# Attention with a relative bias and a mixture of adapters: transposes as 64x64 quadrants, two equal value banks, another order of the work

## The chip, the cores and the metric

The kernel runs on one core of one Trainium2 chip. The time is the device time of one execution in microseconds (us); before the change the median of 3 runs was 206.64 us (206.42 to 207.58). TensorE is the engine for matrix products, VectorE and GpSimd are the engines for elementwise work, ScalarE is the one for exponentials and copies, SyncE issues transfers.

## What is computed

Eight batches of attention with eight heads, 576 positions and a head size of 64, with a bias that depends on the distance of two positions alone and is constant from distance 128 on. Then, for each of the 4608 rows of 512 values, a router picks two of eight adapters of rank 16 and adds their weighted outputs to the row.

```python
scores = scale * q @ k.T + bias_table[bucket(|i - j|)]
attn = exp(scores - max) ; attn = attn / (sum(attn) + 1e-09)
x = (attn @ v) reshaped to rows of 512            # batch, position, (head, d)
logits = x @ w_gate ; topk = the two largest
w = softmax(logits[topk])
out = x + sum over the two of w * ((x @ A[e]) @ B[e])
```

## The kernel before

**Tiling.** A unit is a batch and a pair of heads (`units`, L91); there are 32, four to a batch. Of the 576 positions 512 are the main part, 64 the tail. The 512 queries and keys lie in four chunks of 128, with the position modulo 4 naming the chunk (`load`, L103), so that a key chunk meets the same diagonal band of the bias in each query chunk.

**One unit.** `edges` (L374) makes the scores of tail keys against main queries (two whole-array matmuls, L381) and of main keys against tail queries (16 matmuls of 64x64 tiles, L389), in a tile of two banks, and one exponential (L392). `keys` (L332) makes the scores of one key chunk against 512 queries: four 64x64 tiles of 512 columns (L340), one for each head and each half of the chunk, then four that add the band of the bias (L345); `keys_exp` (L350) takes the exponential of the two banks. Score tiles rotate over three tiles of two banks (`score_tile`, L84). The bias of the edges is multiplied in afterwards (`edge_bias`, L395: GpSimd at L398, VectorE at L401). The values of a unit are made one unit later: `values_b` (L438) for query chunk 3 and the tail, `values_a` (L430) for query chunks 0 to 2; each has a bank of a ring of two (`mp`, L78). A query chunk takes 8 matmuls of 65 columns (64 values and a column of ones that gives the sum of the exponentials, L409) and one of 130 for the tail keys (L416); the tail takes 5 of 130 (L427). `normalise_a` and `normalise_b` (L457, L465) multiply by the reciprocal of the sums and write x.

**Transposes.** q and k of a unit are cast to bf16 (GpSimd, L144) and turned by eight 128x128 transposes into a bank of the ring of two (`transposes`, L297), copied out by VectorE (L305). Tail q and k go through `tail_transposes` (L309), x through `moe_x` (L484), the adapter's product z through `moe_t` (L551), each with a copy of its own.

**Adapters.** For each tile of 128 rows: the product with router and A (`moe_z`, L493), the gate (`moe_g`, `moe_w`, L521, L538; GpSimd and one tanh on ScalarE), the transpose of the gated z, the product with B and the addition of x (`moe_d`, L563, VectorE at L566), the store. A batch has four tiles of main rows, in two groups of two, and every two batches share a fifth for their tails. The adapters of a batch run during the next two batches' units, at places that `moe` (L599) writes down.

**Order.** The order is written out by hand; each engine runs its instructions in the order of the program. The loop over units (L695) emits: loads for unit u + 4 (SyncE), casts for u + 2 and v of u + 1 (`prep`, L666), `edges`, key chunks 0 and 2, an adapter product, `values_b` of u - 1, `values_a` of u - 1, key chunks 1 and 3, transposes of q and k of u + 2 (of u + 1 up to u = 3) and of x. The last unit and the remaining adapter tiles follow as written-out code (L789 on).

Of the kernel before, what the change touches and what calls it, by code (L numbers as in the profile page):

```python
# [14 lines left out]
ALU = mybir.AluOpType  # L15
# [23 lines left out]
def kernel(  # L39
# [34 lines left out]
    ep = ctx.enter_context(tc.tile_pool(name="probs", bufs=2))  # L74
    xp = ctx.enter_context(tc.tile_pool(name="x", bufs=3))
    ms = ctx.enter_context(tc.tile_pool(name="moe_sb", bufs=3))
    xtp = ctx.enter_context(tc.tile_pool(name="xT", bufs=4))
# [6 lines left out]
    def score_tile(name):  # L84
        return scps[next(turns) % 3].tile([128, 2, SM], FP32, name=name, tag="sc")


    TT = 2
    AHEAD = 3
# [5 lines left out]
    NV = 3  # L95
    vts = [cp.tile([128, 4, 2, W1], BF16, name=f"v{i}", tag=f"v{i}") for i in range(NV)]
    tvs = [cp.tile([128, HP, 2 * W1], BF16, name=f"vb{i}", tag=f"vb{i}") for i in range(2)]
    tls = [cp.tile([128, HP, 192], BF16, name=f"tl{i}", tag=f"tl{i}") for i in range(2)]
# [19 lines left out]
    def load_tail(b, names="qkv", g0=0, g1=HP):  # L118
        eng = nc.sync
        for nm in names:  # L120
            src = {"q": q, "k": k, "v": v}[nm][b, :, SM:, :]
            if nm == "v":
                t = stt.tile([128, HP, D], FP32, name="vt", tag="vt")
                for par in range(2):
                    eng.dma_start(out=t[par * 64:(par + 1) * 64, :, :],
                                  in_=src.rearrange("(g two) p d -> two p g d", two=2)[par])
# [20 lines left out]
    def cast_tail(b, nm, eng, g0=0, g1=HP):  # L147
# [6 lines left out]
        for par in range(2):  # L154
            rows = slice(par * 64, par * 64 + 64)
            eng.tensor_copy(tvs[b % 2][rows, :, par * W1:par * W1 + 64], tstage[(b, nm)][rows])
# [20 lines left out]
    for i in range(2):  # L177
        nc.vector.memset(tls[i], 0.0)
# [21 lines left out]
    ELC = cp.tile([128, HP * 192], BF16, tag="ELC")  # L200
    EL = ELC[:, :HP * 128].rearrange("p (g i) -> p g i", g=HP)
    EC = ELC[:, HP * 128:].rearrange("p (g i) -> p g i", g=HP)
    ET = cp.tile([128, HP, 2, 128], BF16, tag="ET")

# [18 lines left out]
    def factors_l():  # L223
        ps = score_tile("fl")
        for hp in range(HP):
            for e in range(2):
                for h in range(2):
                    rows = slice(h * 64, h * 64 + 64)
                    nc.tensor.matmul(_ap(ps[rows, 0, :], hp * 128 + e * 32, [[1, 32], [64, 2]]),
                                     lhsT=Wn[rows, hp, 129 - e:193 - e],  # L230
                                     rhs=turned(h), start=(hp == 0 and e == 0), stop=True,
                                     skip_group_check=True)
                    nc.tensor.matmul(_ap(ps[rows, 1, :], hp * 64 + e, [[2, 32]]),
                                     lhsT=Wn[rows, hp, 1 - e:65 - e],
                                     rhs=turned(h)[:, :32], start=(hp == 0 and e == 0), stop=True,
                                     skip_group_check=True)
        nc.scalar.activation(ELC, ps.rearrange("p a b -> p (a b)")[:, :HP * 192], ACT.Exp,
                             scale=scale)

    def factors_t():  # L240
        ps = score_tile("ft")
        pst = ps.rearrange("p h (g x) -> p h g x", x=64)
        for hp in range(HP):
            for e in range(2):
                for h in range(2):
# [5 lines left out]
        nc.scalar.activation(ET[64:].rearrange("p g c (h i) -> p h (g c) i", h=2), pst[64:], ACT.Exp,  # L251
                             scale=scale)

    def presets():
        for i in range(2):
            nc.gpsimd.memset(tvs[i], 0.0)
            nc.gpsimd.memset(pcs[i], 0.0)
        for i in range(2):
            nc.gpsimd.memset(tvs[i][:64, :, D:W1], 1.0)
            nc.gpsimd.memset(tvs[i][64:, :, W1 + D:], 1.0)  # L260
# [34 lines left out]
    qkT, probs, pva, pvb, xs, xe = ({} for _ in range(6))  # L295

    def transposes(u):  # L297
        ps = mp.tile([128, 2, 4, 128], BF16, name="tp", tag="mm")
        for i, nm in enumerate(("q", "k")):
            n = nat.pop((u, nm))  # L300
            for c in range(4):
                nc.tensor.transpose(ps[:, i, c, :], n[:, c, :, :].rearrange("p h d -> p (h d)"),  # L302
                                    ident)
        sb = qkp.tile([128, 2, SM], BF16, name="qkT", tag="qkT", bufs=3)
        nc.vector.tensor_copy(sb, ps.rearrange("p a c t -> p a (c t)"))  # L305
        qkT[u] = sb


    def tail_transposes(b, gr=None, g0=0, g1=HP):  # L309
        n = nat[(b, "qk")]  # L310
        ps = mp.tile([128, 2 * HP, 128], BF16, name="tq", tag="mm")
        for hp in range(g0, g1):
            nc.tensor.transpose(ps[:, hp, :], n[:, 2 * hp:2 * hp + 2, :].rearrange("p h d -> p (h d)"),
                                ident)
        if gr:
            for c in range(4):
                nc.tensor.transpose(ps[:, HP + c, :], gr.x[0][:, c * 128:(c + 1) * 128], ident)
        t = tls[b % 2][:, g0:g1, :]
        nc.vector.tensor_copy(t[:64, :, :128], ps[:64, g0:g1])
        nc.vector.tensor_copy(_ap(t[64:], 0, [[192, g1 - g0], [128, 2], [1, 64]]),  # L320
                              ps[64:, g0:g1].rearrange("p g (a i) -> p g a i", a=2))
        if gr:
            gr.xT = xtp.tile([128, 1, 4, 128], BF16, name="xT", tag="xT")
            nc.vector.tensor_copy(gr.xT, ps[:, HP:].rearrange("p (n c) t -> p n c t", n=1))  # L324

    def open_probs(u):
        probs[u] = (ep.tile([128, 4, 2, SM], BF16, name="pk", tag="pk"),
                    ep.tile([128, 2 * SM], BF16, name="pt", tag="pt"))

    scs, pcx = {}, {}  # L330

    def keys(u, c):  # L332
# [4 lines left out]
        halves = [(slice(h * 64, h * 64 + 64), slice(f * 64, f * 64 + 64), h, f)  # L337
                  for f in range(2) for h in range(2)]
        for rows, prt, h, f in halves:
# [3 lines left out]
        for rows, prt, h, f in halves:  # L343
            p0, n, y0 = (((0, 64, 32), (0, 96, 0)), ((32, 96, 0), (64, 64, 0)))[g][f]
# [3 lines left out]
        scs[c] = sc  # L348

    def keys_exp(u, c):  # L350
        nc.scalar.activation(probs[u][0][:, c, :, :], scs.pop(c), ACT.Exp, scale=scale)  # L351

    def corners(b, gr=None):
        pz = mp.tile([128, 512], FP32, name="ll", tag="mm")
        ps = pz[:, :HP * 64].rearrange("p (g i) -> p g i", g=HP)
        for hp in range(HP):
            t = tls[b % 2][:, hp, :]
            nc.tensor.matmul(ps[:, hp, :], lhsT=t[:, 64:], rhs=t[:, :64],
                             start=(hp == 0), stop=True, skip_group_check=True)
        if gr:  # L360
            moe_z(gr, 0, pz)
            moe_zc(gr, 0, pz)
            moe_g(gr, 0)
        pcx[b] = ep.tile([128, HP, 64], BF16, name="pcx", tag="pcx")
        nc.scalar.activation(pcx[b], ps, ACT.Exp, scale=scale)

    def corners_bias(b):
        px = pcx.pop(b)
        for h in range(2):
            rows = slice(h * 64, h * 64 + 64)  # L370
            nc.gpsimd.tensor_tensor(pcs[b % 2][rows, :, rows], px[rows], EC[rows], op=ALU.mult)


    def edges(u):  # L374
        b, hp = units[u]
        qT, kT = qkT[u][:, 0, :], qkT[u][:, 1, :]
        tl = tls[b % 2][:, hp, :]
        pt = probs[u][1]
        sc = score_tile("sc")
        for h in range(2):  # L380
            nc.tensor.matmul(sc[:, h, 256:], lhsT=tl[:, 64:],  # L381
                             rhs=_ap(qT, h * 64, [[128, 4], [1, 64]]), start=True, stop=True,
                             skip_group_check=True)
        for c in range(4):
            for f in range(2):
                for h in range(2):
                    rows = slice(h * 64, h * 64 + 64)
                    x0 = c * 128 + f * 64
                    nc.tensor.matmul(sc[f * 64:f * 64 + 64, h, c * 64:c * 64 + 64],  # L389
                                     lhsT=kT[rows, x0:x0 + 64], rhs=tl[rows, :64],  # L390
                                     start=False, stop=True, skip_group_check=True)
        nc.scalar.activation(_ap(pt, 0, [[64, 2], [128, 8], [1, 64]]),  # L392
                             sc.rearrange("p h (x i) -> p h x i", x=8), ACT.Exp, scale=scale)

    def edge_bias(u, eng=nc.vector):  # L395
        b, hp = units[u]
        tl = _ap(probs[u][1], SM + 96, [[128, 4], [1, 32]])
        nc.gpsimd.tensor_tensor(tl, tl, EL[:, hp, :].rearrange("p (c j) -> p c j", c=4),  # L398
# [649 lines left out]
```

## Time and profile before

| | |
|---|---|
| median of 3 runs | 206.64 us (206.42 to 207.58) |
| span of the profiled execution, first to last instruction | 204.3 us |
| granted TensorE clock, mean | 0.993 |
| busy: TensorE, VectorE, ScalarE, GpSimd | 181.9, 146.3, 164.8, 125.3 us |
| TensorE matmul records | 3682 |
| transferred | 39.72 MB, 194 GB/s on average |

The time of the profiled execution itself is not recorded; its span lies 2.3 us under the median, since the time of a run holds what goes before the first instruction and after the last as well. Rows of the profile name a line of the kernel, the engine, the operation, the tiles written and read, the number of instructions, and their busy time. TensorE's rows overlap, because matmuls are pipelined: the distance from one row's start to the next one's tells what a row takes of the engine. `PEld` are its weight loads.

### The profile page before, as it was taken

The numbers are of one execution on the slowest core, as the hardware profiler recorded it, in microseconds if no ns is written. First come the engines' busy times: TensorE is split into PE (matmuls) and PEld (weight loads), VectorE is DVE, ScalarE is ACT, GpSimd is POOL, SyncE is SP. The second block draws the span as 40 slices with busy tenths as digits, with TensorE's granted clock in tenths as the row PEclk, the third lists the DMA queues.
The fourth block names the chain that finished last, engine by engine and source line by source line (L and its number), as shares of the span: only waits on it lengthen the run. The fifth ranks groups of instructions, "written<-read, shape, count | busy, mean of one in ns | idle before, by whom it ended". The sixth has DMA issues, their size and how long they took to land.

```text
span 204.3 us, 8942 instructions
## 1 busy us (share of the span) xinstructions
PE 181.9 (89%) x3682; PEld 129.8 (64%) x3684; DVE 146.3 (72%) x453; ACT 164.8 (81%) x205; POOL 125.3 (61%) x319
## 2 busy tenths in 40 slices
PE   0477898999999989999999989999999899999850
PEld 0245666677767767776677767776677577777630
DVE  5322665677768787889788787888787878888850
ACT  3249688989998897998888879988998869789560
POOL 4293646933858573995849367978577639717020
PEclk9999999999999999999999999999999999999997
DMA  4859798867969487856377999955369932022176
GB/s 136 219 167 277 206 250 247 215 188 225 274 171 273 153 231 187 264 153 200 88 181 242 315 252 254 271 174 163 89 160 299 309 106 106 0 106 107 26 273 219
DMA packets 62113, 39.72 MB, mean 194 GB/s; under 512 B 17896, under 2 KB 59384, under 8 KB 62072
## 3 DMA queue, kind: packets, MB, share of 16 engines
q1 hardware_dynamic: 61272, 38.58, 64.0%
q10 hardware_dynamic: 800, 0.56, 1.1%
q8 instruction: 29, 0.48, 0.9%
q14 instruction: 12, 0.10, 0.2%
HBM read 29.67 MB, written 9.46 MB: 192 GB/s over the span
## 4 chain that ended last, share of the span: by engine, by line
PE 73%; DVE 10%; ACT 6%; DMA 4%; issue 2%; POOL 2%; ACTq 0%; POOLq 0%
PE pv L409 16%; PE sc L340 14%; PE tp L302 8%; PE sc L345 7%; ACT pk L351 5%; PE pv L427 4%; PE dl L565 4%; PE xT_ps L489 3%; PE pv L416 3%; PE pv L496 3%; PE sc L389 3%; PE sc L381 2%; DVE qkT L305 2%; DMA Wt<-g_d 1%; DMA g_d<-gp 1%
## 5 line engine op out<-in xcount | busy, mean ns | idle before, releaser
L351 ACT ACTIVATE pk<-sc 128x1024 bf16<-128x1024 f32 x128 | 124.1, 1027 | 20.8 <-PE sc L345 20.7
L340 PE MATMUL sc<-qkT 64*64 64x512 bf16 x512 | 52.1, 394 | 1.9 <-ACT pk L351 1.3
L409 PEld LDWEIGHTS <-pk 128*128 128x128 bf16 x1024 | 43.6, 98 | 8.7 <-DVE xT L324 2.7
L409 PE MATMUL pv<-v,pk 128*128 128x65 bf16 x992 | 45.5, 193 | 2.3 <-DVE xT L324 1.8
L345 PE MATMUL sc<-Wt,anti 64*64 64x256 bf16 (+1 forms) x512 | 44.1, 301 | 1.1 <-DMA Wt<-g_d 1.0
L392 ACT ACTIVATE pt<-sc 128x1024 bf16<-128x1024 f32 x32 | 32.7, 1023 | 5.1 <-PE sc L389 4.3
L305 DVE COPY qkT<-tp 128x1024 bf16<-128x1024 bf16 x32 | 22.1, 691 | 15.0 <-PE tp L302 14.6
L340 PEld LDWEIGHTS <-qkT 64*64 64x64 bf16 x512 | 18.1, 107 | 15.9 <-issue 5.3
L416 PE MATMUL pv<-vb,pt 128*128 128x130 bf16 x124 | 27.0, 218 | 0.0
L529 POOL TENSOR_TENSOR a<-z,top 128x16 f32<-128x16 f32 (+1 forms) x17 | 3.7, 220 | 34.8 <-DVE top L524 34.5
L144 POOL CAST kn<-ks 128x512 bf16<-128x512 f32 x31 | 19.4, 625 | 5.9 <-DMA ks<-in_k_dram 5.9
L566 DVE TENSOR_TENSOR ot<-dl,xn 128x512 f32<-128x512 f32 x24 | 16.6, 691 | 7.8 <-PE dl L565 7.4
L140 POOL CAST v<-vs 128x512 bf16<-128x512 f32 x32 | 19.9, 623 | 0.0
L345 PEld LDWEIGHTS <-anti 64*64 64x64 bf16 x512 | 18.1, 108 | 1.9 <-issue 1.8
L302 PE MATMUL tp<-ident,qn 128*128 128x128 bf16 x128 | 13.1, 227 | 5.9 <-ACT qn L144 4.9
L461 DVE TENSOR_TENSOR xn<-pv,rc 128x384 bf16<-128x384 f32 x31 | 17.3, 557 | 1.1
L144 POOL CAST qn<-qs 128x512 bf16<-128x512 f32 x27 | 16.5, 611 | 2.2 <-DMA qs<-in_q_dram 1.6
L302 PEld LDWEIGHTS <-qn 128*128 128x128 bf16 x128 | 7.6, 100 | 14.8 <-issue 7.1
L401 DVE TENSOR_TENSOR pt<-pt,ET 64x256 bf16<-64x256 bf16 x32 | 12.1, 377 | 5.0 <-ACT ET L251 3.9
L398 POOL TENSOR_TENSOR pt<-pt,ELC 128x128 bf16<-128x128 bf16 x32 | 13.7, 429 | 2.9 <-ACT pt L392 2.7
L477 DVE TENSOR_TENSOR xe<-pv,rc 64x64 bf16<-64x64 f32 x62 | 13.6, 219 | 0.6
L302 PE MATMUL tp<-ident,kn 128*128 128x128 bf16 x128 | 12.8, 225 | 0.9 <-POOL kn L144 0.9
(158 smaller groups left out, 339.3 us busy)
## 6 DMA issues: line engine op xcount, KB each, us to landing
qs<-in_q_dram SPq DMA_DIRECT2D x32, 256.0 KB, 4.6
vs<-in_v_dram SPq DMA_DIRECT2D x64, 128.0 KB, 3.7
ks<-in_k_dram SPq DMA_DIRECT2D x62, 128.0 KB, 3.8
out_dram<-ot SPq DMA_DIRECT2D x14, 512.0 KB, 3.3
vt<-in_v_dram SPq DMA_DIRECT2D x16, 64.0 KB, 2.9
out_dram<-fot SPq DMA_DIRECT2D x2, 512.0 KB, 3.4
qkt<-in_q_dram SPq DMA_DIRECT2D x7, 128.0 KB, 3.3
qkt<-in_k_dram SPq DMA_DIRECT2D x7, 128.0 KB, 3.6
```

Of the source, the lines that this page charges most:

```text
L140: eng.tensor_copy(t[:, :, :, :D].rearrange("p c h d -> p h c d"), s)
L144: copy(t.rearrange("p c h d -> p h c d"), s)
L302: nc.tensor.transpose(ps[:, i, c, :], n[:, c, :, :].rearrange("p h d -> p (h d)"), ident)
L305: nc.vector.tensor_copy(sb, ps.rearrange("p a c t -> p a (c t)"))
L340: nc.tensor.matmul(sc[prt, h, :], lhsT=kT[rows, c * 128 + f * 64:c * 128 + f * 64 + 64], rhs=qT[rows, :], start=True, stop=False, skip_gro ...
L345: nc.tensor.matmul(_ap(sc[prt, h, :], p0, [[128, 4], [1, n]]), lhsT=turned(h), rhs=_ap(Wt[rows, hp, :], (1 - e) * GY + y0, [[GY, 4], [1, n]]),
L351: nc.scalar.activation(probs[u][0][:, c, :, :], scs.pop(c), ACT.Exp, scale=scale)
L392: nc.scalar.activation(_ap(pt, 0, [[64, 2], [128, 8], [1, 64]]), sc.rearrange("p h (x i) -> p h x i", x=8), ACT.Exp, scale=scale)
L409: nc.tensor.matmul(pv[:, o + h * W1:o + (h + 1) * W1], lhsT=pk[:, c, h, t * 128:(t + 1) * 128], rhs=vm[:, c, h, :], start=(first and h == ...
L416: nc.tensor.matmul(pv[:, o:o + 2 * W1], lhsT=pt[:, SM + t * 128:SM + (t + 1) * 128], rhs=tvs[b % 2][:, hp, :], start=False, stop=False, sk ...
L461: nc.vector.tensor_tensor(_ap(xs[b], hp * 128, [[Dm, 3], [D, 2], [1, D]]), _ap(pv, 0, [[2 * W1, 3], [W1, 2], [1, D]]), _ap(rc, 0, [[2, 3], ...
L566: nc.vector.tensor_tensor(gr.ot[:, t, :], dl, gr.x[t], op=ALU.add)
```

## The change

Line numbers below are those of the kernel after.

- **Transposes** (`turn`, L354). Everything that has to be transposed at one place in a unit (q and k of unit u + 2, tail q and k of a batch, x tiles, gated z) goes into one list. A slot is a 128x128 block as four 64x64 quadrants, each a transpose of its own; up to 16 slots lie in one tile of two banks, which takes a turn of the three score tiles. One copy by VectorE brings all slots to SBUF, where ten such tiles rotate.
- **Edges** (L483). The tail keys against the main queries are four quadrants of 256 columns instead of two whole-array matmuls. The layout of the result changes, so VectorE's and GpSimd's bias products become `edge_t` and `edge_l`; a zero block of 64 columns ahead of each of three permanent tiles lets the tail's products take 128 columns.
- **Values** (L542). Two equal banks: `values(u, j)` makes query chunks j and j + 2, and the tail of head j of the pair as five matmuls of 65 columns. Reciprocal and normalisation are one operation each for a bank (L559, L560). Tail values are loaded and cast to both halves of the partitions.
- **Adapters.** Each row tile has its own store and its own fp32 output tile (8 of them). Groups for the gate are two tiles, or two and the tail tile. The z transposes ride in `turn`. The scores of the tail against itself (`corners`) lie in the free columns of a value bank.
- **Order** (L717). A unit is: loads, casts, `edges`, key chunks 0 and 2, adapter product and values j = 0 of u - 1, edge bias, key chunks 1 and 3, `turn` for u + 2 and the rest, values j = 1 of u - 1. q and k of u + 2 are turned in unit u from the first unit on. Tail loads and casts of a batch come up to two units earlier.
- **End** (L820 on). The last two units make their scores by halves of the queries (`keys_half`, L427: two key chunks against 256 queries) in an interleaved order; the last adapter tiles follow in a new written-out order. x is added for some of them by multiplying its transpose with the identity on TensorE, as before.

```diff
-    def score_tile(name):
+    def score_tile(name, shape=(128, 2, SM), dt=FP32):
+        return scps[next(turns) % 3].tile(list(shape), dt, name=name, tag="sc")
...
-                for par in range(2):
-                    eng.dma_start(out=t[par * 64:(par + 1) * 64, :, :],
-                                  in_=src.rearrange("(g two) p d -> two p g d", two=2)[par])
+                for f in range(2):
+                    eng.dma_start(out=t[f * 64:(f + 1) * 64], in_=src.rearrange("g p d -> p g d"))
...
+    def turn(items):
+        n = sum(k for _, k, _ in items)
...
+        ps = score_tile("tx", (128, 2, 1024), BF16)
+        sb = txp.tile([128, 16, 2, 64], BF16, name="tx", tag="tx")
+        s0 = 0
+        for _, k, src in items:
+            for i in range(k):
+                c = s0 + i
+                for a in range(2):
+                    for h in range(2):
+                        nc.tensor.transpose(ps[h * 64:h * 64 + 64, a, c * 64:c * 64 + 64], src(i, a, h),
+                                            ident[a * 64:a * 64 + 64, a * 64:a * 64 + 64])
+            s0 += k
+        nc.vector.tensor_copy(sb[:, :n], ps.rearrange("p a (c i) -> p c a i", i=64)[:, :n])
...
     def edges(u):
-        for h in range(2):
-            nc.tensor.matmul(sc[:, h, 256:], lhsT=tl[:, 64:],
-                             rhs=_ap(qT, h * 64, [[128, 4], [1, 64]]), start=True, stop=True,
+        for rows, prt, h, f in QUADS:
+            nc.tensor.matmul(sc[prt, h, 256:], lhsT=t[rows, 64:], rhs=qT[rows, f * 256:f * 256 + 256],
+                             start=True, stop=True, skip_group_check=True)
...
+    def pv_tail(u, pv, h, o=260):
...
+        for c in range(4):
+            x0 = 64 + h * SM + c * 64 - par * 64
+            nc.tensor.matmul(pv[:, o:o + W1], lhsT=probs[u][1][:, x0:x0 + 128], rhs=vts[u % NV][:, c, h, :],
+                             start=False, stop=False, skip_group_check=True)
+        nc.tensor.matmul(pv[:, o:o + W1], lhsT=pcs[par][:, hp, :], rhs=tvs[par][:, 2 * hp + h, h, :],
+                         start=False, stop=False, skip_group_check=True)
+
+    def values(u, j):
+        pv = mp.tile([128, 512], FP32, name="pv", tag="mm")
+        pv_main(u, pv, j, range(4))
+        pv_last(u, pv, j)
+        pv_tail(u, pv, j)
+        return pv
...
+    def normalise(u, j, pv):
...
+        nc.vector.reciprocal(rc[:, j, :5], _ap(pv, D, [[W1, 5]]))
+        nc.vector.tensor_tensor(xs[b][:, j, hp], _ap(pv, 0, [[W1, 5], [1, D]]),
+                                _ap(rc, 6 * j, [[1, 5], [0, D]]), op=ALU.mult)
...
+    tturn = {max(4 * c - 4, 2): c for c in range(1, B)}
+    tload = {max(w - 2, 0): c for w, c in tturn.items()}
...
+    for b in range(B - 1):
+        w = 4 * (b + 1)
+        for i in range(4):
+            at(xt, w + i, (x_item, b, i))
+            at(za, w + 1 + i, (b, i))
+            at(xt, w + 3 + 2 * (i // 2), (zt_item, b, i))
+            at(da, w + 4 + i, (b, i))
...
-    for u in range(NU - 1):
+    for u in range(NU - 2):
         open_probs(u)
         if u:
             prep(u)
+        if u in tload:
+            load_tail(tload[u])
...
         if u + 4 < NU:
             load(u + 4)
         edges(u)
         for c in KO[:2]:
             keys(u, c)
...
         if u:
...
+            step(u - 1, 0, da.pop(u, []), z=zs[0], zt=ta.pop(u, [None])[0])
...
+            edge_l(u)
+            edge_t(u)
         for c in KO[2:]:
             keys(u, c)
...
+        items.append(qk_item(u + 2))
+        if u in tturn:
+            items.append(tl_item(tturn[u]))
+        for fn, bb, i in xt.pop(u, []):
+            items.append(fn(tile_for(bb, i)))
+        turn(items)
         if u:
...
+            step(u - 1, 1, db.pop(u, []), z=zs[0], zt=tb.pop(u, [None])[0], corner=tcorner.get(u))
...
+    halves_of(U0, (0, 0), (0, 1))
+    step(U0 - 1, 0, [(L - 2, 2)], z=(L - 1, 1))
...
+    edges(U1)
+    halves_of(U1, (0, 0))
...
+    turn([x_item(T(L - 1, 2)), x_item(T(L - 1, 3))])
+    step(U0 - 1, 1, [(L - 2, 3)], z=(L - 1, 2))
...
+    halves_of(U1, (0, 1))
+    halves_of(U0, (1, 0))
+    step(U0, 0, [(L - 2, 4)], z=(L - 1, 3))
+    halves_of(U0, (1, 1))
+    halves_of(U1, (1, 0))
+    turn([zt_item(T(L - 1, 0)), zt_item(T(L - 1, 1))])
+    moe_w(groups[(L - 1, 2)])
...
+    halves_of(U1, (1, 1))
+    turn([zt_item(T(L - 1, 2)), zt_item(T(L - 1, 3)), x_item(T(L, 0)), x_item(T(L, 1))])
+    step(U0, 1, [(L - 1, 1)])
```

`step` emits the adapter products that are due, the values of a bank with router products and corner scores in its free columns, the normalisation, and the copies of what the bank holds besides.

More of the change, by code (lines that the diff above doesn't have):

```diff
@@ L309, in tail_transposes @@
-    def tail_transposes(b, gr=None, g0=0, g1=HP):
-        n = nat[(b, "qk")]
[L311 to L324, printed above, removed]
+    halves = (NU - 2, NU - 1)
@@ L633, with step @@
+    def step(u, j, ds=(), z=None, zt=None, corner=None):
+        for t in ds:
+            moe_d(tile_of(*t))
+        pv = values(u, j)
+        if z:
+            moe_z(tile_of(*z), pv)
+        if zt:
+            ps = moe_t(tile_of(*zt), pv)
+        if corner:
+            corners(*corner, pv)
+        normalise(u, j, pv)
+        if z:
+            moe_zc(tile_of(*z), pv)
+        if zt:
+            moe_tc(tile_of(*zt), ps)
     cast(0, "q", nc.scalar)
@@ L804 @@
+    step(U0, 1, [(L - 1, 1)])
+    zj = bank()
+    for i in range(2):
+        zsum(zj, i, T(L, i), range(HP), i == 0)
+    zcopy(groups[(L, 0)], zj, dve)
+    turn([x_item(T(L, 4)), x_item(T(L, 2), 0, 3), x_item(T(L, 3), 0, 3)])
+    s0 = next(turns)
     scx.close()
@@ L952 @@
-    rows4 = out[(B - 1) * S:(B - 1) * S + SM, :].rearrange("(p c) n -> p c n", c=4)
-    for i in range(2):
-        values(i, KO[3])
-    for i in range(2):
-        norm(i)
-    vx = turn(4, 1, bank(-1), (2, 3))
-    tall = turned16(bank(2), 2)
-    for t in range(2):
-        nc.tensor.transpose(tall[:, t, :], g1.zt[:, t, :, :].rearrange("p e r -> p (e r)"), ident)
-    act(g1.zT, tall)
-    z01, z23 = cut(bank(5), 2, ER + E), cut(bank(0), 2, ER + E)
-    for i in range(2):
-        zsum(z01, i, i, range(HP - 2))
```

954 lines of the change are left out of this document (408 added, 546 removed).

## The prediction

> **What bounds the kernel now.** First the page: span, busy shares, the chain by engine.
> ```profile
> span 204.3 us, 8942 instructions
> ...
> PE 181.9 (89%) x3682; PEld 129.8 (64%) x3684; DVE 146.3 (72%) x453; ACT 164.8 (81%) x205; POOL 125.3 (61%) x319
> ...
> PE 73%; DVE 10%; ACT 6%; DMA 4%; issue 2%; POOL 2%; ACTq 0%; POOLq 0%
> ```
> TensorE holds 73% of the chain that ends last; ScalarE is nearly as busy (81%) but holds 6%. The table by stretches comes next; I cut it where the score matmuls of units 5, 12, 16, 20, 24, 28 and 30 begin (a unit is a batch and a head pair, 0 to 31) and where the last exponential ends (189.08).
> ```profile
> core 0: us, PE busy (x) PEld busy (x) DVE busy (x) ACT busy (x) POOL busy (x), PEclk, DMA share, GB/s
> 41.31:78.50 37.19, 36.34 (x788) 26.66 (x786) 28.53 (x89) 33.36 (x40) 22.88 (x54) 1.00 0.75 213
> 78.50:100.48 21.98, 21.81 (x449) 15.31 (x447) 18.39 (x57) 19.93 (x26) 17.73 (x45) 1.00 0.61 190
> 100.48:122.40 21.92, 21.32 (x457) 15.59 (x455) 17.58 (x54) 18.89 (x24) 13.37 (x33) 1.00 0.82 235
> ...
> 144.37:166.29 21.92, 21.32 (x456) 15.59 (x455) 17.58 (x54) 18.87 (x24) 13.35 (x33) 1.00 0.78 223
> 166.29:177.92 11.63, 11.32 (x235) 8.16 (x232) 9.45 (x29) 10.88 (x14) 9.48 (x25) 1.00 0.12 48
> 177.92:189.08 11.16, 11.16 (x238) 7.99 (x236) 9.37 (x31) 9.68 (x13) 4.66 (x16) 1.00 0.25 98
> 189.08:204.30 15.22, 7.07 (x91) 5.04 (x89) 6.80 (x27) 6.07 (x16) 1.64 (x6) 0.90 0.50 174
> ```
> A batch of four units takes 21.92 to 21.98 us, 5.48 a unit, with TensorE busy 21.3 to 21.8 of it at the full clock and ScalarE 18.9 to 19.9. Units 5 to 28 take 166.29 - 41.31 = 124.98 us (5.43 each). So the middle is set by TensorE's own work. The start times of one unit on TensorE show what that work is (a row's second column is an overlapped duration; what counts is the distance from row to row):
> ```profile
> 100.48 0.38 PE L381 MATMUL sc<-qkT,tl 128*128 128x256 bf16 x2
> 100.80 0.32 PE L389 MATMUL sc<-tl,qkT 64*64 64x64 bf16 x16
> 100.94 0.39 PE L340 MATMUL sc<-qkT 64*64 64x512 bf16 x4
> 101.16 0.33 PE L345 MATMUL sc<-Wt,anti 64*64 64x256 bf16 x4
> 101.27 0.44 PE L340 MATMUL sc<-qkT 64*64 64x512 bf16 x4
> ...
> 101.75 0.39 PE L565 MATMUL dl<-Bc,zT 128*128 128x512 bf16 x1
> 101.98 0.42 PE L409 MATMUL pv<-v,pk 128*128 128x65 bf16 x8
> 102.24 0.22 PE L416 MATMUL pv<-vb,pt 128*128 128x130 bf16 x1
> 102.29 0.40 PE L427 MATMUL pv<-v,pt 128*128 128x130 bf16 x4
> ...
> 102.58 0.40 PE L496 MATMUL pv<-AW,xT 128*128 128x136 bf16 x4
> 102.92 0.42 PE L409 MATMUL pv<-v,pk 128*128 128x65 bf16 x8
> ...
> 103.86 0.22 PE L558 MATMUL pv<-ident,zt 128*128 128x128 bf16 x1
> 104.01 0.41 PE L340 MATMUL sc<-qkT 64*64 64x512 bf16 x4
> ...
> 104.84 0.40 PE L302 MATMUL tp<-ident,qn 128*128 128x128 bf16 x4
> ...
> 105.30 0.61 PE L489 MATMUL xT_ps<-ident,xn 128*128 128x128 bf16 x8
> 105.75 0.38 PE L381 MATMUL sc<-qkT,tl 128*128 128x256 bf16 x2
> ```
> Edge scores 0.46 (100.48 to 100.94), two key chunks 0.81 (to 101.75), adapter output 0.23, values and router 0.94 (to 102.92), values and one transpose 1.09 (to 104.01), two key chunks 0.83, transposes of q and k 0.46 (eight, 57 ns each), of x 0.45 (in two units of four). Two prices follow. A pass from whole-array to 64x64 work costs a pause: a whole-array matmul of 130 columns takes 0.055 (102.24 to 102.29), one of 128 from 103.86 to 104.01 0.15, so 0.09 is the pause. And 16 quadrant matmuls of 64 columns, each with a weight load of its own, take 100.80 to 100.94: 0.036 for four that lie side by side.
>
> ScalarE over the same unit:
> ```profile
> 101.22 1.02 ACT L392 ACTIVATE pt<-sc 128x1024 bf16<-128x1024 f32 x1
> 102.14 1.94 ACT L351 ACTIVATE pk<-sc 128x1024 bf16<-128x1024 f32 x2
> ...
> 104.62 1.94 ACT L351 ACTIVATE pk<-sc 128x1024 bf16<-128x1024 f32 x2 [0.55 <-PE sc L345]
> ```
> Five exponentials, 0.92 apart (101.22 to 102.14; 1.94 for two of 1.02), and 0.55 idle until TensorE delivers. The exponential of the chunk begun at 104.01 starts at 104.62, 0.26 after TensorE is through with it (chunk: 0.35).
>
> **The change part by part, per unit in the middle.** *Transposes.* One slot is four 64x64 quadrants in place of one 128x128. The nearest row is L389: same tile form, own weights in every quadrant, 64 columns, so 0.036 a slot against 0.057. L302's transposes cost what L416's plain matmul does (0.055), so a transpose has no price of its own. A unit turns 8 slots of q and k, 4 to 8 of x, and adapter and tail slots, 14.6 on average: 0.53, with 0.04 for the pass back 0.57. Taken away: 0.46 + 0.25 (4.5 of x) + 0.06 (zT) + 0.06 (tail). Bounds of a slot: 0.031 (64 columns at the pace of L409, 65 columns in 0.0325) and 0.107, one whole weight load:
> ```profile
> L340 PEld LDWEIGHTS <-qkT 64*64 64x64 bf16 x512 | 18.1, 107 | 15.9 <-issue 5.3
> ```
> Loads last 0.107, yet four with their matmuls take 0.036: they hide. The Trainium skill, TensorE: Matmul & The Clock Gate, section LDWEIGHTS (loading the stationary operand), gives a load columns / 1.2 ns, an estimated 53 ns for 64; a slot paced by it would make the unit 5.18 and the time about 200, by the row it is 194.3.
> *Edge scores.* Two whole-array matmuls of 256 columns become four quadrants beside each other: 0.11 (the L345 row of 256 columns, 101.16 to 101.27) instead of 0.31 with the pause in it; with 0.15 for L389 and the 0.09 pause 0.35. *Values.* Two equal banks: 16 x 0.0325 + 2 x 0.055 + 5 x 0.033 = 0.80 each; the tail products are ten of 65 columns instead of five of 130 (+0.05). With router (0.24) and pause the first is 1.13, the second 0.85 with corners and the tail's router. *Keys* stay: 0.81 and 0.79 (no pass behind the second pair). TensorE's sum: 0.35 + 0.81 + 0.23 + 1.13 + 0.79 + 0.57 + 0.85 = 4.73.
>
> *A new wait.* The transposes go to a two-bank tile of the ring of three score tiles, so six take turns: edges, c0, c2, c1, c3, turned tile. The turned tile takes c2's place and waits for c2's exponential. From the first edge matmul: edge exponential at 0.35 + 0.25 = 0.60; c2's starts 2 x 0.915 later and ends after 1.02; release 0.06: 3.51. TensorE alone would be there at 0.35 + 0.81 + 0.23 + 1.13 + 0.79 = 3.31. Behind the waiting transpose stand the second value bank and the next unit's edge scores, for which ScalarE waits: 3.51 + 0.57 + 0.85 = **4.93 a unit**. ScalarE's own sum is 5 x 0.915 + 0.19 (a tanh, half a corner exponential) = 4.77, so it doesn't bound, but it is the floor. I take 4.93; lower end 4.77.
>
> *VectorE.* A unit's copies out of transposes become one of 14.6 x 128 = 1870 elements, and four operations normalise it instead of six.
> ```profile
> L305 DVE COPY qkT<-tp 128x1024 bf16<-128x1024 bf16 x32 | 22.1, 691 | 15.0 <-PE tp L302 14.6
> L461 DVE TENSOR_TENSOR xn<-pv,rc 128x384 bf16<-128x384 f32 x31 | 17.3, 557 | 1.1
> L566 DVE TENSOR_TENSOR ot<-dl,xn 128x512 f32<-128x512 f32 x24 | 16.6, 691 | 7.8 <-PE dl L565 7.4
> ```
> At L305's rate (0.15 + 0.53 ns an element, the 0.15 as in the two fp32 rows) 1.13 us; against 0.69 + some 0.8 in the smaller copies now; with the two operations less VectorE's 18.39 / 4 = 4.6 a unit falls to an estimated 4.2, under 4.93. The copy ends 0.25 + 1.13 after the turn, the second bank's reciprocal and normalisation 0.67 after that: 0.3 before the next first bank wants its place. The corner exponential now reads that bank too and VectorE waits for it with the output additions behind; it is short of that 0.3, cost nothing while the cover lasts, at most 0.27 in two units of four.
>
> *GpSimd and DMA.* The tail's v is loaded and cast twice, outputs leave by tile. GpSimd is at 17.7 of 22 us at most, and its casts of q and k end before 3.5 in the unit; SyncE has waits to give:
> ```profile
> SPq L582 <- DVE rc L468: 33.9, 9, 11.4
> ```
> Counted as nothing; without that cover 16 further issues of 0.64 (L125's row, below) would be 10 us.
>
> *Start.* q and k of unit u+2 are turned at the end of unit u from the first unit on (now one unit later up to u = 3), so arrival counts:
> ```profile
> 27.52 0.61 POOL L144 CAST kn<-ks 128x512 bf16<-128x512 f32 x1 [2.98 <-DMA ks<-in_k_dram]
> ...
> 32.95 0.61 POOL L144 CAST kn<-ks 128x512 bf16<-128x512 f32 x1 [0.87 <-DMA ks<-in_k_dram]
> ...
> 36.41 0.61 POOL L144 CAST kn<-ks 128x512 bf16<-128x512 f32 x1
> ```
> k of units 4 and 5 is cast by 28.13 and 33.56: edge scores of units 3 and 4 not before 29.3 and 34.7 (cast, turn 0.3, values 0.85). The tail load of batch 2 now stands ahead of load 6, four issues of 0.64,
> ```profile
> 39.61 1.28 SPq L125 DMA_DIRECT2D vt<-in_v_dram  x2
> ```
> so k of unit 6 comes at 37.0 + 2.6 = 39.6, less what it lay ready (about 0.1), and unit 5 starts at 39.5 + 0.57 + 0.85 = 40.9 instead of 41.31. I take 0.4 gained; ends: 3 lost, 2 gained.
>
> *End.* Today unit 30's edges start at 177.92, the last exponential ends 11.16 later, the last addition (next row) at 198.07, +20.15, the span at +26.4.
> ```profile
> 197.38 0.69 DVE L1016 TENSOR_TENSOR fol<-f,xe 128x512 f32<-128x512 f32 x1 [0.27 <-PE f L916]
> ```
> New: the same ten exponentials, ending at +11.2 by the prices above. Then, as estimates from these prices: wait for the adapter's gate (tanh behind the ninth exponential, three GpSimd steps) to 11.2, ten slots, the last bank of unit 30 and router 2.4, second turn, outputs of batch 6 and routers 2.4, to 16.0; second half of unit 31 normalised, turned, routed 1.9, gate 1.5, turned and multiplied 1.2, copied 0.6; the tail tile behind it 1.2: +22.3. Stores 5.5 (6.2 now, with 512 KB pieces): +27.8, **1.4 lost**; ends 1 gained, 4 lost.
>
> *Sum.* 40.9 + 25 x 4.93 + 27.8 = 192.0 of span against 204.3. What lies around the span: median 206.64 less 204.3 is 2.3 (the runs reach from 206.42 to 207.58). 192.0 + 2.3 = **194.3 us**.
>
> **The rivals.** *ScalarE's floor*, if release and turn are shorter than I take them: 4.77, 25 x 0.16 = 4 less, 190.3. For it: only 0.16 apart. *Weight loads set the slot.* If a quadrant's load hides only half behind the quadrants before it (0.107 / 2), a slot is 0.053, a unit 4.93 + 14.6 x 0.017 = 5.18, the time 200.5; against it stands L389 with its 0.036. This is what the section on LDWEIGHTS above comes to.
>
> *The copy runs at the fp32 rate* (reads 64 elements from one bank, then from the other): (691 - 557) / 128 = 1.05 ns an element, 2.1 us. Then the loop turn, copy, normalise, next first bank, keys, turn is 0.53 + 0.25 + 2.1 + 0.67 + 0.06 + 1.92 = 5.53 a unit: 209.3. Against it: L305 reads the same type from PSUM.
>
> *Slower: the quadrants don't overlap their loads.* Place: every turn. Price: 0.107 a slot, the weight-load row; 4.93 + 14.6 x 0.071 = 5.97 a unit, 220.3. It decides from 0.07 a slot, where 12.3 us / 25 units is used up. For it: never is there a run of more than 16 quadrants in L389, and a turn has up to 64; against it: within the 16 no slowing is seen. The Trainium skill has a rule for this on the same page, section "Wait — 56ns, not 53.3ns?": however small, matmuls start no less than some 25 ns apart, an estimate of 100 ns a slot, with a time near this rival's. The trace disagrees: L389's 16 start within 0.15.
>
> **How the numbers follow.** Forecast 0.67; ScalarE's floor 0.10; half-hidden loads 0.07; slow copy 0.08; quadrants in a row 0.08. The likeliest gives 194.3. The range goes from the floor with an even end (188.5) to half-hidden loads with the worst start (204); that leaves out the last two cases and some of the rest. A measurement here tells 0.5% from nothing. Slow copy and quadrants come in degrees: of their 0.16 I count 0.02 faster, 0.03 within 0.5%, 0.11 slower. So faster 0.67 + 0.10 + 0.07 + 0.02 = 0.86, same 0.03, slower 0.11.
>
> **What would show it.** Right: slots of 0.031 to 0.04 in the turn, units of 4.8 to 5.05 us, TensorE waiting for ScalarE ahead of the turn, copies of 1.0 to 1.25, unit 5 near 41, about 28 us from unit 30 on. Wrong: slots over 0.05, copies near 2, TensorE waiting for VectorE ahead of a value bank, or for casts in the middle; an end of over 31 us.

## The result, and the profile after

The changed kernel takes **213.32 us** (median of 4 runs, 212.76 to 214.36), the kernel before 206.53 in the same comparison: a ratio of 1.033 (95% interval 1.029 to 1.037), slower by far more than the 0.5% that a measurement can tell. The forecast was 194.3, its range 188.5 to 204. Some runs fall into a slower state: the times and ratios below are of fast runs, but the profiles of e1_whole, e4_before_split and e9_fewer_elsewhere are of slow ones, 1.5 to 1.6% above the fastest of their kernel.

The profiled run took 213.37 us. From its page, the span, TensorE's line and the queue that brings instructions (packets, MB, share):
```profile
span 211.5 us, 12203 instructions
...
PE 171.7 (81%) x5399; PEld 132.6 (63%) x5399; DVE 129.6 (61%) x327; ACT 164.1 (78%) x204; POOL 124.0 (59%) x303
...
q8 instruction: 42, 0.69, 1.3%
```
Before, TensorE had 3682 matmuls and was busy 89% of the span; now it has 5399 and is busy 81%. Instructions come by DMA: 0.69 MB / 42 is 16 KB a packet, and 5399 matmuls with 5399 weight loads, each an instruction, are some 42 times 256; such 256 are called a block from here on. Before there were 29 packets for 3682 and 3684. The table by stretches, cut where the edge scores of units 5 and 30 begin:
```profile
42.26:182.43 140.17, 125.33 (x4085) 96.89 (x4084) 96.13 (x234) 122.34 (x151) 90.58 (x208) 0.99 0.70 204
182.43:211.50 29.07, 18.61 (x504) 14.47 (x501) 17.07 (x50) 13.94 (x23) 8.75 (x31) 0.95 0.33 111
```
The start took 42.26 (forecast 40.9), the middle 140.17 (25 x 4.93 = 123.25), the end 29.07 (27.8): 1.4, 16.9 and 1.3 over. So the miss lies in the middle, where TensorE stood still for 14.8 us (140.17 less 125.33; before 2.7). What it waited for, over the whole run (us in total, times, longest; "issue": nothing that the profile shows):
```profile
PE sc L422 <- issue: 4.7, 3, 2.5
PE sc L494 <- issue: 4.2, 3, 2.6
...
PE tx L365 <- ACT pk L425: 1.4, 4, 0.4
...
PE pv L520 <- issue: 1.2, 4, 0.4
PE sc L417 <- issue: 0.9, 1, 0.9
...
PE pv L520 <- DVE xn L560: 0.7, 2, 0.4
...
PE aw L285 <- issue: 0.6, 1, 0.6
```
Those on buffers and engines, which the prediction had thought of, are small. The issue rows that fall into the middle come to 12.1 us in 14 stops, with the smaller ones that aren't shown; the kernel before has none. The longest stop, in the order of instructions on TensorE (start, duration of the group; the bracket is the idle time before it):
```profile
106.40 0.30 PE L489 MATMUL sc<-tx 64*64 64x256 bf16 x4
106.53 0.22 PE L494 MATMUL sc<-tx 64*64 64x64 bf16 x5
109.31 0.28 PE L494 MATMUL sc<-tx 64*64 64x64 bf16 x11 [2.55 <-issue]
...
110.73 0.61 PE L616 MATMUL dl<-Bc,tx 128*128 128x512 bf16 x1
111.13 1.09 PE L520 MATMUL pv<-v,pk 128*128 128x65 bf16 x16
112.03 0.40 PE L528 MATMUL pv<-vb,pt 128*128 128x130 bf16 x2
```
The stretch behind the stop in the table by stretches (the clock stands behind the engines' columns):
```profile
109.31:113.10 3.79, 3.79 (x56) 2.62 (x56) 0.69 (x1) 2.86 (x3) 3.25 (x6) 0.55 0.32 97
```
TensorE stops in the middle of 16 like matmuls, all free to run: 5 are issued, then nothing for 2.55 us, then 11. Behind it the matmuls are slow as well: sixteen value products take 0.90 (111.13 to 112.03) where they take 0.51 elsewhere (100.24 to 100.75, below); the granted clock from 109.31 to 113.10 is 0.55. This isn't so behind every long stop: behind that of 2.48 us before 168.42 the clock was 1.00 (168.42 to 172.20). Where do the stops stand? The same table, cut at seven of them, counts the matmuls and weight loads in between:
```profile
69.17:86.00 16.83, 15.21 (x512) 11.73 (x513) 12.18 (x30) 14.54 (x18) 10.62 (x28) 1.00 0.84 246
86.00:109.31 23.31, 19.79 (x642) 15.31 (x642) 16.22 (x38) 19.58 (x24) 16.14 (x38) 1.00 0.77 215
109.31:127.74 18.43, 16.67 (x513) 12.93 (x514) 11.67 (x29) 15.75 (x19) 11.15 (x24) 0.91 0.67 191
127.74:141.39 13.65, 12.37 (x384) 9.31 (x385) 9.72 (x24) 12.52 (x15) 7.89 (x19) 1.00 0.73 210
141.39:163.05 21.66, 19.81 (x641) 15.13 (x642) 16.29 (x38) 18.84 (x24) 14.26 (x34) 1.00 0.74 217
163.05:168.42 5.37, 2.90 (x128) 2.43 (x129) 1.97 (x4) 3.21 (x5) 3.58 (x11) 1.00 0.74 228
```
Matmuls and loads together: 1025, 1284, 1027, 769, 1283, 257, which are 4, 5, 4, 3, 5 and 1 times 256, but for a few at the edges. Each stop is the end of a block of instructions: **the next one was not there yet**. In the trace's record of transfers the packet of that next block (1.0 us) starts 0.3 to 3.5 us after the block ahead was begun, 1.6 on the mean, and its instructions run 1.15 us after its end at the earliest. From the packet of 45.98 to that of 185.78, 32 further, a block takes 4.37 us; 327 instructions a unit (8169 in the row 42.26) / 256 x 4.37 = 5.58, the 5.61 measured. That counts the same blocks once more and proves nothing by itself; the experiments below do. Before it was one packet in 6.2 us.

### The profile page after: what moved, and what is told of

Same layout as the page of the kernel before. It is cut to its first block, busy times and chain, and to the rows that moved or that the text cites. A ratio compares the mean times of both kernels' runs of the same rounds, so it can differ in the third digit from the quotient of the medians.

```text
span 211.5 us, 12203 instructions
## 1 busy us (share of the span) xinstructions
PE 171.7 (81%) x5399; PEld 132.6 (63%) x5399; DVE 129.6 (61%) x327; ACT 164.1 (78%) x204; POOL 124.0 (59%) x303
## 5 line engine op out<-in xcount | busy, mean ns | idle before, releaser
L425 ACT ACTIVATE pk<-sc 128x1024 bf16<-128x1024 f32 x120 | 114.5, 1031 | 12.5 <-PE sc L422 12.3
L417 PE MATMUL sc<-tx 64*64 64x512 bf16 x480 | 50.9, 403 | 1.0 <-issue 0.9
L422 PE MATMUL sc<-Wt,anti 64*64 64x256 bf16 x480 | 43.4, 309 | 6.7 <-issue 4.7
L368 DVE COPY tx<-tx 128x2048 bf16<-128x2048 bf16 (+8 forms) x36 | 36.3, 1009 | 18.5 <-PE tx L365 18.1
L560 DVE TENSOR_TENSOR xn<-pv,rc 128x320 bf16<-128x320 f32 x62 | 30.5, 491 | 2.1
L559 DVE RECIPROCAL rc<-pv 128x5 f32<-128x5 f32 x62 | 11.9, 192 | 22.9 <-PE pv L567 13.7
L417 PEld LDWEIGHTS <-tx 64*64 64x64 bf16 x480 | 16.9, 109 | 10.8 <-issue 2.8
L365 PEld LDWEIGHTS <-qn 64*64 64x64 bf16 x512 | 11.1, 112 | 14.5 <-ACT qn L141 4.9
L537 PE MATMUL pv<-v,pt 128*128 128x65 bf16 x248 | 18.0, 195 | 0.2 <-issue 0.2
L528 PE MATMUL pv<-vb,pt 128*128 128x130 bf16 x124 | 17.5, 224 | 0.0
L494 PE MATMUL sc<-tx 64*64 64x64 bf16 x512 | 11.3, 196 | 4.2 <-issue 4.2
L537 PEld LDWEIGHTS <-pt 128*128 128x128 bf16 x256 | 14.2, 99 | 0.4 <-issue 0.4
```

The costliest lines, as they stand in the source:

```text
L365: nc.tensor.transpose(ps[h * 64:h * 64 + 64, a, c * 64:c * 64 + 64], src(i, a, h), ident[a * 64:a * 64 + 64, a * 64:a * 64 + 64])
L368: nc.vector.tensor_copy(sb[:, :n], ps.rearrange("p a (c i) -> p c a i", i=64)[:, :n])
L417: nc.tensor.matmul(sc[prt, h, :], lhsT=kT[rows, c * 128 + f * 64:c * 128 + f * 64 + 64], rhs=qT[rows, :], start=True, stop=False, skip_gro ...
L422: nc.tensor.matmul(_ap(sc[prt, h, :], p0, [[128, 4], [1, n]]), lhsT=turned(h), rhs=_ap(Wt[rows, hp, :], (1 - e) * GY + y0, [[GY, 4], [1, n]]),
L425: nc.scalar.activation(probs[u][0][:, c, :, :], sc, ACT.Exp, scale=scale)
L537: nc.tensor.matmul(pv[:, o:o + W1], lhsT=probs[u][1][:, x0:x0 + 128], rhs=vts[u % NV][:, c, h, :], start=False, stop=False, skip_group_che ...
```

## The experiments

*Theory:* the change put so many instructions into a unit that their blocks arrive late. *Rivals:* the long runs of transposing quadrants themselves hold TensorE; the waits between engines set the unit; every instruction has a price. Times stand beside the kernel before on the same chip.

**e1_whole.** One whole-array transpose a slot:
```
+    nc.tensor.transpose(ps[:, c, :], src(i, 0, None), ident)
-    for a in range(2):
-        for h in range(2):
-            nc.tensor.transpose(ps[h*64:h*64+64, a, c*64:c*64+64], src(i, a, h), ident[...])
```


> The changed kernel with one whole-array transpose a slot in place of four quadrants (in the few turns that hold a tail tile the quadrants stay; the heads of a value bank lie side by side so that a slot is one operand). TensorE has 8382 instructions in place of 10800. Theory (instructions arrive too late: blocks of 256, some 4.3 us apart at best): 262 instructions a unit take longer to run than to fetch, so the waits for nothing at every 256th instruction go, although the transposes themselves get dearer by 14.6 x 0.021 = 0.3 us a unit: units of 5.1 to 5.3, 200 to 206 us. Rival (the added waits between the engines set the unit, the missing instructions only follow): the unit grows by the 0.3, 214 to 221 us.

204.95 us, ratio 0.992 (0.989 to 0.995): 0.8% under the kernel before, 8 us faster than the change. Units of 5.22 (4.93 and the 0.3 of the dearer slots), 32 packets, and the waits for nothing are down to 0.3 us. The theory's figures came.

**e2_rows.** Two transposes of 64 rows by 128 columns a slot:
```
+    nc.tensor.transpose(ps[:, a, c*64:c*64+64], src(i, a, None), ident[pr, pr])
-    for h in range(2): ... (64 by 64)
```


> The changed kernel with two transposes of 64 rows by 128 columns a slot in place of four quadrants, into the same two banks (tail tiles keep quadrants). 9020 TensorE instructions in place of 10800, 282 a unit. Theory (late instructions): 282 instructions are fetched in some 4.7 us, under the unit's 4.93: nearly all waits for nothing go, 197 to 205 us. Rival (waits between engines): the columns, banks and copies are those of the changed kernel, so 211 to 215 us.

200.44 us, 0.972 (0.968 to 0.975). The middle, and eight slots in it behind the last bias (q from 71.97, k up to 72.20):
```profile
44.01:169.77 125.76, 119.28 (x3372) 92.68 (x3390) 96.63 (x234) 121.11 (x151) 90.39 (x208) 1.00 0.77 224
```
```profile
71.67 0.33 PE L426 MATMUL sc<-Wt,anti 64*64 64x384 bf16 x4
71.97 0.29 PE L366 MATMUL tx<-ident,qn 64*128 64x64 bf16 x8
...
72.20 0.30 PE L366 MATMUL tx<-ident,xn 64*128 64x64 bf16 x8
```
0.23 for eight, 0.029 a slot, like the quadrants' 0.031, with half the instructions. The middle takes 125.76, 5.03 a unit; waits for nothing fall to 0.8 us. The columns, banks and copies are those of the change, and so is the order of the work, so these don't make it slow.

**e3_noload.** `load` issues nothing for units over 5.

> The changed kernel; the loads of q, k and v of units 6 to 31 are left out (their casts read what units 2 to 5 loaded), all else is kept, all 10800 TensorE instructions too. If the instruction blocks come late because they queue behind the data: each block's packet starts within 0.8 us of the block before being taken up, and the waits for nothing vanish or fall under 2 us in all, 195 to 201 us. If the fetch is slow by itself: the packets start as late as before (1.4 us on the mean) and the waits stay, 207 to 214 us. If the waits between the engines set the unit: DMA waits are 1 us in all, 211 to 214 us.

202.95 us, 0.982 (0.977 to 0.988). All 10,800 instructions are there, yet the middle is 127.94 and the waits for nothing come to 3.0 over the run (12.5 in the change), the largest row being the one below:
```profile
43.01:170.95 127.94, 120.27 (x4065) 95.61 (x4084) 96.76 (x234) 121.41 (x151) 90.54 (x208) 1.00 0.23 70
```
```profile
PE sc L425 <- issue: 1.1, 2, 0.9
```
This lies between the first two expectations: counted by the weight loads, the packets start 1.1 us after the block ahead on the mean (1.6 in the change), and the late ones, up to 3.5, are gone (2.2 at most). Most of the loss needs the data traffic (70 GB/s here, 204 in the change); the fetch isn't quick without it.

**e4_before_split.** The other way round, in the kernel before:
```
+    for x in range(0, SM, SM // 4):
+        for rows, prt, h, f in halves:
+            nc.tensor.matmul(sc[prt, h, x:x+128], lhsT=..., rhs=qT[rows, x:x+128], ...)
-        nc.tensor.matmul(sc[prt, h, :], lhsT=..., rhs=qT[rows, :], ...)
```


> The kernel before with its key scores cut into smaller matmuls: four of 128 columns for each one of 512, two bias matmuls for each one; same columns, same results, no wait, copy or tile changed. TensorE has 11466 instructions in place of 7370, 358 a unit. Theory (late instructions): 358 / 256 blocks x 4.3 us = 6.0 us a unit in place of 5.43, waits for nothing at every 256th instruction, 215 to 228 us. Rival (waits between engines, instructions arrive in time): the same columns take the same time, 206 to 209 us.

218.27 and 219.48 us, 1.060 (1.055 to 1.065). A chunk's sixteen matmuls of 128 columns take 0.23 (84.28 to 84.51 in the trace), as four of 512 did, and still:
```profile
PE sc L342 <- issue: 3.5, 5, 1.3
PE pv L413 <- issue: 3.4, 3, 1.7
PE sc L349 <- issue: 2.6, 5, 0.7
```
The kernel before now has the change's fault without any part of the change, 383 matmuls and 383 loads from the stop at 85.2 to the one at 98.1 (three blocks). Units of 6.01. Stops make up 8.6 us of the 13.6 by which the middle is longer than before (150.17 against 136.61); the rest I only put down to what they upset, it wasn't taken apart.

**e5_keys_rows** and **e6_all_rows** take instructions out of the key scores, by tiles of 64 by 128:
```
+    for h in range(2):
+        nc.tensor.matmul(sc[:, h, :], lhsT=kT[rows, c*128:c*128+128], rhs=qT[rows, :], ...)
-    for rows, prt, h, f in QUADS: ... (64 by 64)
```


> The changed kernel with its turned tiles as they are (quadrants), but the key scores and the key half of the edge scores as products of 64 rows by 128 columns instead of pairs of quadrants: 9808 TensorE instructions, 306 a unit. Theory (late instructions, wherever they stand): 306 / 256 blocks x 4.1 to 4.4 us = 4.9 to 5.25 a unit, 199 to 207 us. Rival (long runs of transposing quadrants themselves hold TensorE up): the runs are as long as before, 211 to 215 us.

> The kernel of e2_rows (transposes of 64 by 128) with the key scores and the key half of the edge scores as 64 by 128 as well: 8028 TensorE instructions, 251 a unit. Theory (a threshold: instructions cost only where their blocks come late): e2_rows had no late block left, so 198 to 201 us, as e2_rows. Rival (every instruction has a price, as from the changed kernel to e2_rows 12.9 us for 1780 = 7 ns): 992 fewer give 7 us, 193 to 194 us.

214.43 (1.041, 1.037 to 1.045) and 216.10 us (1.048, 1.045 to 1.050): both outside the theory, the first within its rival's 211 to 215; yet hardly a stop is left (0 and 0.2 us in all), and the turn that the rival blames takes e5_keys_rows as long as the change (0.64 a unit up to the values behind it, on the mean). Two chunks of e6_all_rows, then of e2_rows:
```profile
102.38 0.39 PE L422 MATMUL sc<-tx 64*128 64x512 bf16 x2
102.70 0.36 PE L426 MATMUL sc<-Wt,anti 64*64 64x256 bf16 x4
102.99 0.39 PE L422 MATMUL sc<-tx 64*128 64x512 bf16 x2
```
```profile
71.11 0.41 PE L421 MATMUL sc<-tx 64*64 64x512 bf16 x4
71.35 0.33 PE L426 MATMUL sc<-Wt,anti 64*64 64x256 bf16 x4
71.46 0.44 PE L421 MATMUL sc<-tx 64*64 64x512 bf16 x4
```
A chunk takes 0.61 (102.38 to 102.99) instead of 0.35 (71.11 to 71.46): scores of 64 by 128 and bias of 64 by 64 now follow each other, with a pause at each pass from one tile form to the other. On the mean of units 5 to 29 it is 0.10 from scores to bias, four times a unit, and 0.18 from bias to the next scores, twice: 0.75 more a unit, some of it won back elsewhere, so that units take 5.57 and 5.61 where e2_rows has 5.03. The prediction had a price like that (0.09) for whole-array tiles and I didn't apply it here, so the pair says nothing between theory and rival.

**e7_rows_cast**, **e12_rows_cast_again.** In e2_rows TensorE waits in unit 4:
```profile
PE aw L285 <- POOL A L277: 2.8, 1, 2.8
```
The edit puts `weights_cast()` ahead of `prep(3)`.

> The kernel of e2_rows with the casts of the adapter's weights put ahead of unit 3's other casts on GpSimd (there TensorE waits 2.8 us for them in unit 4, as they stand behind a cast that waits for a load). The start is then bound by the casts of k alone: unit 5 at 41.5 to 42.5 in place of 44.0, 198 to 199.5 us. If the load of the tail or of the weights is what comes late, the wait only moves: 200 to 201 us.

> The kernel of e7_rows_cast once more in five rounds, as it is the quickest so far: 198 to 200.5 us, a ratio to the kernel before of 0.960 to 0.972; its start ahead of e2_rows by 1 to 2.8 us.

197.97 to 200.80 us in three runs (0.967, 0.959 to 0.974) and **199.72 us (0.966, 0.963 to 0.968)**, the quickest of all that compute the whole result. The wait is gone; unit 5 starts at 41.2 in one profile, at 42.7 in the other, so the gain over e2_rows (some 0.5% by the ratios) isn't settled.

**e8_before_split2.** The cut of e4_before_split in two instead of four, bias whole.

> The kernel before with each key score matmul of 512 columns cut into two of 256: 8394 TensorE instructions in place of 7370, 262 a unit. Theory (threshold): a unit of 5.43 us takes up a block in 5.3 us, a block can be had in some 4.3: no wait, 206 to 208 us. Rival (every instruction has a price, 13.9 us for 4096 in e4_before_split): 3.5 us more, 210 us.

206.67 us, 1.002 (1.0005 to 1.003): 1024 more instructions cost nothing that counts, and no wait without a releaser appears. There is a threshold, not a price for each: at the pace of the kernel before (5.46 a unit) this one needs 48 instructions a us, e4_before_split 66.

**e9_fewer_elsewhere.** What e5_keys_rows should have been:
```
+    for rows, prt, h, f in QUADS:
+        nc.tensor.matmul(sc[prt, h, :256], lhsT=kT[rows, f*64:f*64+64], rhs=qT[rows, :256], ...)
-    for c in range(4): ... (16 of 64 columns)
+    nc.tensor.matmul(pv[:, h*130:h*130+130], lhsT=pk_slice(u, c, h, j), rhs=(both heads), ...)
-    for f in range(2): ... (two of 65 columns)
```


> The changed kernel with its turns as they are (quadrants), but fewer instructions elsewhere, tile forms kept: the key half of the edge scores as 4 quadrants of 256 columns in place of 16 of 64, the main value products as 8 of 130 columns in place of 16 of 65 (which leaves out the right operands: these scores and half of the probabilities are not the reference's). 9008 TensorE instructions, 281 a unit, columns as before. Theory (late instructions, wherever they stand): as e2_rows, 282 a unit: no wait at every 256th instruction, 199 to 204 us. Rival (long runs of transposing quadrants hold TensorE up, and 64 by 128 is only a quicker form): the turns are as they were, 211 to 215 us.

198.12 and 200.72 us, 0.964 (0.957 to 0.970), units of 5.03, with every turn as in the change; the largest row without a releaser is
```profile
PE sc L422 <- issue: 0.7, 2, 0.4
```
So the quadrant runs of the turn are harmless; it is the count.

**e10_run_quiet**, **e11_run_loaded.** The fetch by itself:
```
+    for i in range(2048):
+        nc.tensor.transpose(run[pr, (i//2 % 16)*64:(i//2 % 16)*64+64], anti[pr, pr], ident[pr, pr])
```


> The kernel of e7_rows_cast, and behind its last matmul a run of 2048 transposes of 64 by 64 that wait for nothing (the quadrants at rows 0 to 63 and 64 to 127 in turn), 16 blocks of instructions, while the loads are over. TensorE alone would need some 0.015 us a transpose, 1.9 us a block. Theory: a block is had only every 3.5 to 4.1 us (packet 1.1, start of the next one after some 1.4, 1.3 until it runs), so the run takes 56 to 66 us, with a wait at every 256th instruction. Rival (blocks are fetched well ahead, and the waits came from something else in the loop): 29 to 40 us for the run, no waits.

> As e10_run_quiet, with the loads of q and k of all units issued once more beside the run (16 MB that nothing reads). If the blocks queue behind data: 4.3 to 6 us a block, the run 70 to 96 us. If the fetch has a fixed pace: as in e10_run_quiet within 3 us.

The transposes in order, quiet and loaded (the idle time before each group in brackets):
```profile
220.94 2.21 PE L950 MATMUL fm<-ident,anti 64*64 64x64 bf16 x128 [0.78 <-issue]
224.40 2.21 PE L950 MATMUL fm<-ident,anti 64*64 64x64 bf16 x128 [1.24 <-issue]
228.12 2.21 PE L950 MATMUL fm<-ident,anti 64*64 64x64 bf16 x128 [1.52 <-issue]
```
```profile
234.14 2.65 PE L952 MATMUL fm<-ident,anti 64*64 64x64 bf16 x128 [2.06 <-issue]
238.96 3.60 PE L952 MATMUL fm<-ident,anti 64*64 64x64 bf16 x128 [2.18 <-issue]
```
128 matmuls and their 128 loads, then a wait, at 13 of the 16 crossings quiet and 15 loaded. (Where the quiet run has none, the block ahead ran at a lower granted clock and took up the time itself.) Each was run once. The quiet run lasts 56.6 us (194.49 to 251.11), 3.54 a block; the loaded one 69.3 (192.72 to 262.06; 70 to 96 were expected), 4.33 a block at some 260 GB/s. That is 72 and 59 instructions a us. Quiet, a packet starts 1.15 us after the block ahead has begun, takes 1.05 and is followed by its instructions 1.38 later; loaded it is 1.88, 1.16 and 1.38, so it is mainly the start of the packet that the data delays. The granted clock, 0.78 on the mean in the loaded run (hence groups of up to 3.6 us), isn't the cause: four blocks amid the loads that ran wholly at 1.00 were followed by the next after 4.27 to 5.10 us. The changed kernel at the forecast's pace would need 8169 in 123.25 us, 66: more than the loaded rate, less than the quiet one, which fits e3_noload. e2_rows took 54 (6762 in 125.76), the kernel before 41.

## Why the prediction was wrong, point by point

- **Slot and turn: right.** In the change a turn and the bank behind it begin so:
```profile
99.49 0.33 PE L422 MATMUL sc<-Wt,anti 64*64 64x384 bf16 x4
99.66 0.29 PE L365 MATMUL tx<-ident,qn 64*64 64x64 bf16 x16
99.78 0.30 PE L365 MATMUL tx<-ident,kn 64*64 64x64 bf16 x16
99.91 0.27 PE L365 MATMUL tx<-ident,zt 64*64 64x64 bf16 x8
...
100.24 0.67 PE L520 MATMUL pv<-v,pk 128*128 128x65 bf16 x16
100.75 0.28 PE L528 MATMUL pv<-vb,pt 128*128 128x130 bf16 x2
```
Eight slots in 0.25 (99.66 to 99.91), 0.031 each (forecast 0.036); this turn of 14 slots takes 0.58 with the pass back (forecast 0.57 for 14.6). So neither half-hidden loads nor quadrants in a row came, and none of the other rivals either.
- **Copy and VectorE: right.**
```profile
L368 DVE COPY tx<-tx 128x2048 bf16<-128x2048 bf16 (+8 forms) x36 | 36.3, 1009 | 18.5 <-PE tx L365 18.1
```
1.01 us on the mean against 1.13; VectorE is busy 96.13 / 25 = 3.85 a unit against 4.2.
- **TensorE's unit: near in size where blocks are in time**, but not by the wait that I named, so the 4.93 owes something to luck. In e2_rows and e12_rows_cast_again units take 4.7 to 5.9, 5.03 and 5.04 on the mean. The turn hardly ever waits for c2's exponential (1.4 us in all in the change, row above; 0.4 in the middle of e2_rows): there TensorE is busy 119.28 / 25 = 4.77 a unit (my sum was 4.73), and the rest is short waits for several things.
- **The step that failed: "25 x 4.93" in the sum.** It added what TensorE does with its instructions and let their arrival count for nothing, without saying so. A unit holds 327 instructions, 225 before (5629 in units 5 to 29); a rise by 45% should at least have been a rival. Of the signs that I had named for being wrong, only TensorE waiting for VectorE ahead of a value bank came, 0.7 us in all. Of the 16.9, 12.1 are the stops; about 2.5 is the unit of 5.03; by an estimate 1.7 is the lower clock behind the stop before 109.31 (0.45 of 3.79); the remaining 0.6 stays open.
- **Start:** 1.4 later, and TensorE waits 1.5 in unit 4 for the cast of the adapter's weights, which I had not counted; with the casts ahead unit 5 began at 41.2 and 42.7, so the wait for loads may decide as well.
- **End:** the last addition ends 24.93 behind unit 30's edges (206.67 + 0.69, below), not 22.3; the stores behind it took 4.1, not 5.5. TensorE first, then VectorE:
```profile
194.53 0.25 PE L365 MATMUL tx<-ident,zt 64*64 64x64 bf16 x8 [1.32 <-POOL zt L602]
```
```profile
199.98 0.18 DVE L880 RECIPROCAL frc<-fm 128x4 f32<-128x4 f32 x1 [1.22 <-PE fm L528]
...
206.67 0.69 DVE L304 TENSOR_TENSOR ot<-f,xn 128x512 f32<-128x512 f32 x1 [0.70 <-PE f L796]
```
The gate holds the turn until +12.1 (forecast 11.2), unit 31's second half is normalised from +17.5 (16.0), and from there to the last addition's end are 7.4 (6.3): each stretch a little too short. (My terms for the end add up to 22.4, not 22.3, and those of the floor with an even end to 188.9, not 188.5; neither matters here.)

## What to carry to other kernels

Count the instructions of the busiest engine for each stage, not only their durations: beside heavy loads a block of 256 on TensorE came every 4.3 us here, so a stage that needs more than some 59 matmuls and weight loads a us isn't paced by its work. Cut work into small tiles only as far as that, prefer the form with fewer instructions where it has the same pace (64 by 128 for 64 by 64), and count the passes between tile forms, which cost 0.10 to 0.18 each in e6_all_rows. Idle rows with no releaser, at distances that are multiples of 256 matmuls and weight loads, are the mark of late blocks.

## What the runs showed of the hardware

- TensorE's instructions came in 16 KB packets of 256, which started only 0.3 to 3.5 us after the block ahead had begun, and ran 1.15 us or more after the packet's end. A block came every 3.54 us without other traffic and every 4.33 beside some 260 GB/s (one run each). The Trainium skill, Runtime: NRT & Kernel Launch, section Instruction fetch mechanics, has the blocks of 256 and a fetch of the next while the current one runs; that agrees. That the crossing is mostly hidden, as it says, held at 41 instructions a us and failed where 66 were needed.
- After a stop of 2.55 us the granted clock was 0.55 for 3.8 us; after another of 2.48 us it stayed at 1.00.
- A transpose of 64 rows by 128 columns takes as long as the two quadrants in its place (a slot of two or of four: 0.029 and 0.031).
- A pass between 64 by 128 and 64 by 64 tiles cost about 0.13 (0.61 less 0.35 for two; or the last bias up to the turn, 0.30 from 71.67 to 71.97 in e2_rows against 0.17 from 99.49 to 99.66 with quadrants), near the 0.09 to whole-array tiles.
